# Transposes of q and x on TensorE in halves of eight blocks instead of transposing transfers, and all sums of w_in in group 0

## The chip, the cores and the metric

The kernel runs on one core of a Trainium2 chip. The metric is the device time of one execution in microseconds (us), as the median of several runs. Inside the core, TensorE (PE in the profile, its weight loads PEld) multiplies, VectorE (DVE) and ScalarE (ACT) work on elements, GpSimd (POOL) fills and casts, SyncE (SP) issues most transfers. Each engine takes its own instructions in order; semaphores tie them together.

## The reference

A linear attention with 8 batches, 8 heads, 576 tokens and 64 features a head, and on its output a feed-forward layer with tanh-GELU:

```python
def phi(x):
    return np.where(x > 0, x, np.exp(x) - 1.0) + 1.0
q_p, k_p = phi(q), phi(k)
kv = np.einsum('bhsd,bhse->bhde', k_p, v)
z = np.sum(k_p, axis=2)
num = np.einsum('bhsd,bhde->bhse', q_p, kv)
den = np.einsum('bhsd,bhd->bhs', q_p, z)[..., None] + 1e-06
attn_out = num / den
...
x = attn_out.transpose(0, 2, 1, 3).reshape(4608, 512)
h = x @ w_in                                  # w_in: 512 x 2048
g = 0.5 * h * (1.0 + np.tanh(c * (h + 0.044715 * h * h * h)))
return g @ w_out                              # w_out: 2048 x 512
```

All inputs and the output are float32.

## The kernel before

**Groups.** The 4608 tokens are nine groups of 512. Groups 0 to 7 are the first 512 tokens of the eight batches, four chunks of 128; group 8 is the 64 tokens that are left of each batch ("rest"). `iteration(j)` computes the feed-forward layer of group j and, meanwhile, the attention of group j + 1 and the maps of q and k of batches after it. The order of everything in a group is written out by hand, a string for each group, `ORDER_A` (group 0) to `ORDER_I` (group 8), read word by word. All instructions of an engine stand in the order of these words.

**The words that matter.** `p3` is a plain product for a block of 128 of the 2048 features (4 matmuls of 512 columns) and `g3` its GELU; `X`, `Y`, `Z`, `W` with a number or a letter are the steps of a `Quad`, a product of two by two blocks with seven instead of eight multiplications (matmuls of 256 columns), where `1` to `7` are products on TensorE, `s`, `m`, `u` copies out of PSUM, `c` and `a` additions and `g11` to `g22` GELUs; `o1` to `o7` are the same for w_out, 16 matmuls of 256 columns each, with `os`, `om`, `ou`, `oc..` for their copies and additions; `S1:0-8` are sums of g on VectorE; `n2` is the attention of chunk 2 of the next group: four matmuls of transposed q with the batch's 64x65 blocks of k and v, then a reciprocal and a multiplication on VectorE (`divide`, L290), which leaves a chunk of x with tokens on partitions; `k3` sums k times v for batch 3; `!qe:4`, `!qx:4`, `!qm:4` are the three parts of phi for q of batch 4 (exponential on ScalarE, linear part and minimum on VectorE), `!ke`, `!kx`, `!km` the same for k, `!re`, `!rx`, `!rm` for the rest; `!vc` casts v; `!lq`, `!lk`, `!lv`, `!lr` start loads; `!xs` takes the four sums of the next group's x on VectorE (`sum_x`, L979); `!w0` to `!w3` take the four sums of w_in for the blocks of quad X, Y, Z or W (`sum_w_in`, L956, four VectorE instructions of 512 columns each). A prime moves a copy to the other of ScalarE and VectorE.

**Transposes before.** TensorE contracts over partitions, so q must stand with features on partitions for the attention and x for the product with w_in. Batches 0 and 1 are transposed by TensorE (`transpose_q`, L405 and L510, and `transpose_x`, L346: a matmul of each 128x128 block with an identity, and a copy of PSUM to SBUF). For batches 2 to 7, the rest, and x of groups 2 to 8, `least_q` (L619), `least_rest` (L565) and `transposed_x` (L641) issue transfers from SP that transpose a chunk of 128x512 each: 24, 4 and 28 of them. They stand in SP's queue among the loads, which SP takes in order.

**Buffers.** A pool of seven load buffers (tag `ld`) holds q, k and v of a batch, the float32 weights before their cast, and later three tiles that stay: A and B, which hold sums of w_out and of w_in for the blocks of quads W and X (`begin_sums`, `more_sums`, words `!bq` and `!mq` in group 1), and `rows` (`!br` in group 2). Quads Y and Z have their sums in `w_near`. w_in's sums are taken in group 0 for Y and Z (`!w1`, `!w2`) and at the head of group 3 for X and W (`!w0`, `!w3`). PSUM has six single banks (tag `b`) for all products and TensorE transposes, and one pair (tag `a`) for the attention.

**Group 0.** `first_batch` (L395) brings batch 0 to its x with filler matmuls (`warm`) in between. POOL casts w_in and most of w_out to fp16 as their loads land. `plan_second` (L496) puts batch 1 between the products of group 0: at slot 15 of `ORDER_A` its maps (`maps`, L500), at slot 23 its transposes of q, at 27 its k times v, at 29 to 35 the attention and the transposes of x.

Of the kernel before, what the change touches and what calls it, by code (L numbers as in the profile page):

```python
# [17 lines left out]
def kernel(  # L18
# [9 lines left out]

# [6 lines left out]
    P = 128  # L39
# [40 lines left out]
    def bank(name, shape, dt=FP32):  # L80
        return ps_b.tile(shape, dt, name=name, tag="b")
# [3 lines left out]

# [65 lines left out]

    nc.scalar.preload_act_table_set("exp_and_others")
# [9 lines left out]
    for i in (2, 1, 3):  # L162
        load_w_in(i)
    load_w_out(0)
# [17 lines left out]

    warm = pg.tile([P, 512], BF16, name="warm", tag="g")
    nc.vector.memset(warm, 0.0)
    ident = pth.tile([P, P], BF16, name="ident")
    make_identity(nc, ident)
    vps = [pkv.tile([P, J * NP, E], BF16, name=f"vp{i}") for i in range(2)]
    ident_x = pth.tile([P, P], FP16, name="ident_x")
    t_sum = pth.tile([P, 3, KM // 2, MAIN // 2], FP16, name="t_sum")
    kvbds = [pkv.tile([P, NP, 2 * E], BF16, name=f"kvbd{b}") for b in range(B)]  # L190
    make_identity(nc, ident_x)
    for i in range(2):
        nc.gpsimd.memset(vps[i][:, :, D:E], 1.0)
    for t in kvbds:
        nc.gpsimd.memset(t, 0.0)

# [4 lines left out]

    phi, exps, own = {}, {}, {}
# [44 lines left out]

# [137 lines left out]
    def xt_chunk(j, c):  # L385
        return xts[j][:, :, P * c : P * (c + 1)]
# [5 lines left out]

# [90 lines left out]

# [12 lines left out]
    def plan_second():  # L496
# [3 lines left out]
        def maps():  # L500
            for n in "qk":
                exp_of(n, b)
            cast_w_out(2, nc.scalar.copy, slice(0, 2))
            linear_of("q", b)
            sum_w_out(slice(0, 1))
            linear_of("k", b)
            for n in "qk":
                least_of(n, b)
# [56 lines left out]
    def least_rest(m):  # L565
        least_of("qr", m)
        if m == 0:
            qts[B] = pt.tile([P, C, NP, P], BF16, name="qt")
        nc.sync.dma_start_transpose(
            out=qts[B][:, m], in_=phi["qr", m][:, 0].rearrange("p h d -> p (h d)")  # L570
        )
# [5 lines left out]
    def load_rests(i):  # L577
# [32 lines left out]
        "bq": lambda j: begin_sums(),  # L610
        "mq": lambda j: more_sums(),
# [7 lines left out]
    def least_q(b, cs=slice(0, C)):  # L619
        least_of("q", b, cs=cs)  # L620
        if b not in qts:
            qts[b] = pt.tile([P, C, NP, P], BF16, name="qt")
        for c in range(cs.start, cs.stop):
            nc.sync.dma_start_transpose(
                out=qts[b][:, c],
                in_=phi["q", b][:, c].rearrange("p h d -> p (h d)"),
            )
# [13 lines left out]
    def transposed_x(b, c, x):  # L641
        if b not in xts:
            xts[b] = pt.tile([P, NP, MAIN], FP16, name="xt")
        nc.sync.dma_start_transpose(out=xt_chunk(b, c), in_=x)

    x_parts = {}

    def attention_piece(b, c, in_banks=False):

        if b < B:  # L650
            return transposed_x(b, c, (nab_in_banks if in_banks else nab)(qts[b], b, c))
# [27 lines left out]
        transposed_x(b, c, x)  # L679
# [36 lines left out]


# [205 lines left out]
    FIRST_BLOCK = (0, 2, 4, 6)  # L923
    def sums_at(u, t):
        own["sums"][u] = t.rearrange("p (u n c) f -> p u n c f", u=1, c=KM // 2)
        own["w"][u] = own["sums"][u][:, 0]

    own["w"], own["sums"] = {}, {}
    for u in (1, 2):
        sums_at(u, w_near[:, u])  # L930

    def begin_sums():

        own["A"] = pld.tile([P, MM + 2, N2], FP16, name="w_sum", tag="ld")
        sums_at(3, own["A"][:, MM // 2 : MM])

    def more_sums():

        own["B"] = pld.tile([P, MM + 2, N2], FP16, name="w_more", tag="ld")
        own["qr", 0] = own["B"][:, MM:].rearrange("p a n -> p (a n)").bitcast(BF16)  # L940
        sums_at(0, own["B"][:, MM // 2 : MM])

# [122 lines left out]
    def iteration(j):  # L1065
# [10 lines left out]
        for word in ORDERS[j].split():  # L1076
# [27 lines left out]
            elif kind == "k":  # L1104
                kv_in_pair(int(name))
            elif kind == "S":
# [4 lines left out]
            elif kind == "!":  # L1111
                what, _, b = name.rstrip("'").partition(":")
                if what == "vc":
                    cast_v_of(int(b), name.endswith("'"))
                elif b:
                    prepare_of[what](int(b))
                else:
                    prepare[what](j)
# [5 lines left out]
        "p0 g0 p1 g1 p2 g2 p3 g3 p8 g8 p9 g9 p10 g10 p11 g11 !w1 p4 g4 p5 g5 p6 g6 p7 g7 p12 g12 "  # L1124
        "p13 g13 p14 g14 p15 g15 !w2 @15 o0:0-4 o1:0-4 o2:0-4 o3:0-4 o0:4-8 o1:4-8 o2:4-8 o3:4-8 "
        "@23 o0:8-10 o1:8-10 o2:8-10 o3:8-10 @27 o0:10-12 o1:10-12 @29 o2:10-12 o3:10-12 o0:12-16 "
        "@32 o1:12-16 @33 !qe:2 o2:12-16 @34 o3:12-16 @35"
    )
    ORDER_B = (
        "p0 !ke:2 p13 !lk:3 p1 !kx:2 !vc:2' !km:2 !t !qx:2 @2 p7 !qm:2 p2 g0 !bq !lv:3 !mq g1 g2 "  # L1130
        "p3 g3 k2 !a0 !a2 !a3 p6 p4 p5 p8 g4 p11 g5 !kxb:3 p9 g6 g7 T0-8 o1 os' g8 g9 p10 !qx:3 "
        "!kxa:3 g10 p12 o7 !lk:4 g11 p14 g12 g13 om S1:0-6 p15 S2:0-5 g14 g15 n1' o2 S1:6-8 "
        "S2:5-8 S4:0-6 n0 oc11' o6 !qe:3 n3' ou S4:6-8 !ke:3 n2 o5 oc22 !lq:4 !km:3 !vc:3 o4 oc21 "
        "o3 oc12' !qm:3 !ke:4 !xs !kx:4"
    )
    ORDER_C = (
        "!br k3 @1 Y1 Z1 !km:4 p6 Zs p0 !lk:5 !t g6 !lv:4 Z2 Zg11 Z6 p14 Z7 p8 Zu Z5 Zm g14 p7 g0 "
        "g8 Ys p15 !qx:4 Zc g7 Y6 Yu' Zg22 Y2 Yg11 Y7 Ym Z4 Za g15 n1 p1 g1 Y5 Yc Zg21 Y4 Ya Z3 "
        "Zg12 S1:4-8 n3 o1 Yg22 S2:4-8 p9 S1:0-1 S2:0-1 n2 Yg21 os g9 Y3 Yg12 S1:1-3 S1:3-4 "
        "S2:1-3 S2:3-4 S3:0-8 !qe:4 n0' o2 !lv:5 !qm:4 o6 oc11 ou o7 om o5 !kx:5 S4:0-8 oc22 "  # L1140
        "!ke:5 !vc:4 !xs o4 oc21 o3 !km:5 k4 oc12"
    )
    ORDER_D = (
        "!lq:5 !w0 Z1 X1 !t Y7 Y1 Xs X2 !w3 X7 @1 Ym' X6 Xg11 Ys n1 Xm' Y2 X4 Y6 Xu Xa X5 Yg11 Zs "
        "Xc Yu Xg21 n0 !lk:6 Y4 !vc:5' Z6 Zu X3 Xg12 Z2 Ya Y5 W1 Z7 Yc Zg11 Ws k5 Xg22 Zm Yg21 W6 "
        "Wu' Z5 Yg22 Y3 Yg12 !lv:6 Zc W7 Wm' W2 Z4 Za W5 Zg22 Z3 Wc W4 Wa n3 Wg11 Zg12 Zg21 o1 "
        "S1:0-6 Wg21 n2 os W3 Wg12 S2:0-6 !lq:6 Wg22 S1:6-8 S2:6-8 o2 !qe:5 S3:0-5 o6 S3:5-8 o7 "
        "S4:0-8 !qx:5 ou !qm:5 om !ke:6 oc11 o5 !lk:7 oc22 !vc:6 !kx:6 o4 o3 oc21 !xs oc12'"
    )
    ORDER_E = (  # L1150
        "X1 X7 Xm Xs Y7 !t X6 X2 Xg11 Xu' @1 Y1 Ym X4 X5 Ys Xa Xg21 Z1 Y2 Yg11 Zs !lr:0 Y4 Xc X3 "
        "!km:6 Y6 Yu n2 Z7 Xg12 Z6 Ya Z2 Zu Xg22 Yg21 n1 Zm W1 Z5 Y5 Yc Zc Zg11 Ws k6 Z4 Yg22 W7 "
        "Za Z3 Wm' Zg22 W6 Wu' n3 W4 Zg12 W2 Wg11 Wa Y3 W5 Wc Yg12 S1:0-6 S2:0-6 Zg21 Wg21 o1 os "
        "n0 Wg22 W3 Wg12 S1:6-8 S2:6-8 S3:0-8 !qx:6 o2 !lv:7 S4:0-8 !qe:6 o6 ou !lq:7 oc11 o7 om "
        "!xs o5 oc22 !re:0 o4 !re:1 !ke:7 !qm:6 oc21 !kx:7 o3 oc12'"
    )
    ORDER_F = (
        "!t !km:7 X1 Y1 Y7 !vc:7' Xs Ym' X6 X7 @1 X2 Xu Y4 Xm' !lr:1 X5 Xc X4 Xa Xg11 Ys k7 Y6 "
        "Yu' Y2 Xg22 Xg21 X3 Z1 Yg11 Zs !qx:7 Y5 W1 Yc Z2 Xg12 Ya Zg11 Z6 Zu Ws' Y3 Z7 Zm n1 Yg12 "
        "Z5 Yg22 W6 Wu S1:0-2 W7 Z4 W2 W5 Wm' Zc !rx:0 Zg22 Z3 Zg12 Wc Wg11 n0 Wg22 W4 S1:2-6 "  # L1160
        "S3:0-6 W3 Wg12 o1 os S1:6-8 S3:6-8 S2:0-8 n3 !qe:7 o7 om' o6 Wa Za Zg21 Yg21 ou' n2 o4 "
        "!qm:7 S4:0-6 o5 oc22 Wg21 o2 !rm:0 oc11 S4:6-8 o3 oc21 oc12 !xs"
    )
    ORDER_G = (
        "X1 n0 !rx:1 !rm:1 Xs Y7 Ym' X7 Xm' X2 X6 Xu' Xg11 Y1 Ys X4 Xa n2 X5 Y2 Z1 Xg21 Y6 Y4 "
        "Yg11 Zs W1 Xc Xg22 Yu' Ya !rx:2 X3 Xg12 Yg21 Y5 @1 Z6 Yc Z2 Z7 Zg11 Zu' Ws' Y3 Z5 Yg22 "
        "W7 Wm' W2 Wg11 Yg12 Zm Zc W6 Wu' W4 Zg22 Wa Z3 Zg12 Z4 W5 Za Zg21 Wc S1:0-6 o1 Wg21 "
        "S2:0-6 os n1 W3 Wg22 Wg12 S1:6-8 S2:6-8 S3:0-8 n3' o2 !rx:3 o6 o7 oc11' !re:2 ou S4:0-8 "
        "om o5 !re:3 !rm:2 oc22 o4 oc21 !rm:3 o3 !xs oc12' !t"
    )  # L1170
    ORDER_H = (
        "X1 Xs X7 Xm' n0' n1 X6 Xu X2 Xg11 X4 Y1 Xa X5 Y7 Xc Ys Y6 Xg21 Y2 Yg11 Yu' Z1 X3 W1 Zs "
        "Y5 Z6 Z2 Xg12 Ym Yc Y4 @1 Z7 Zu' Z5 Xg22 Zg11 Ya Y3 Ws W6 W2 Zm Yg21 Zc W7 Yg22 Wu' Wm "
        "Zg22 Wg11 Z3 Zg12 W5 Z4 Za Yg12 Zg21 Wc Wg22 W4 Wa S1:0-6 o1 os W3 Wg21 S2:0-6 Wg12 "
        "S1:6-8 S2:6-8 S3:0-8 n2 n3' o2 oc11 o6 ou o7 om o5 S4:0-8 o4 oc22 !xs o3 oc21 oc12'"
    )
    ORDER_I = (
        "X1 Y7 Ym X7 Xm Xs X2 Xg11 @1 X6 Y1 X4 Z1 Ys Y6 Xu' Xa Xg21 Y2 Y4 Yg11 Zs X5 Yu' Ya Y5 "
        "Yg21 Z7 Z2 Z6 W1 Xc Xg22 Zg11 Yc Y3 Yg22 Zu' X3 Ws' Z5 W6 Zm Zc Yg12 Wu W2 W7 W5 Wg11 Wm "
        "Zg22 Wc Xg12 Z4 Za Z3 Zg12 W4 Wa W3 Wg12 S1:0-6 S2:0-1 Wg22 o1 S1:6-8 S2:1-8 S3:0-8 o5 "  # L1180
        "Zg21 o6 Wg21 S4:0-8 o7 o2 o4 o3"
# [36 lines left out]
```

## Time and profile before

| | |
|---|---|
| median of 3 runs | 265.94 us (265.37 to 266.69) |
| the profiled execution | 266.18 us, its span 264.4 us |
| TensorE clock granted | 1.0 throughout |
| transposing transfers of x (28) | 2.3 us to landing |
| transposing transfers of q (24) | 4.1 us to landing |
| read from HBM, written | 36.70 MB, 9.44 MB |

The span runs from the first to the last instruction in the trace; the time of an execution is a little longer. Busy times of the engines add up over the span, and an engine that waits is not busy. The transfer engines are busy for 93 to 105% of the first 60 us, when the weights and the first batches come in at 348 to 405 GB/s in stretches of 20 us.

### The profile page before, as it was taken

The page shows a single profiled execution, that of the slowest core. Times are in us where ns is not written, and L with a number is a line of the kernel's source. Part 1 is how long each engine was busy: PE and PEld are TensorE (multiplying, and loading weights), DVE is VectorE, ACT ScalarE, POOL GpSimd, SP SyncE. Part 2 cuts the span into 40 slices and gives each one's busy share as a digit, 9 for nine tenths or more (in the row PEclk, how much of TensorE's full clock was granted, in tenths as well). Part 3 has the DMA queues.
Part 4 walks back from the last instruction along what each step waited for, and adds up shares of the span by engine and source line. Part 5 has one row for each costly group of instructions (what it writes and reads, how often), then busy time and mean ns, then how long its engine had stood idle before and what let it go on. Part 6 is the DMA issues. An engine that isn't in the chain of part 4 may idle for free. (4 is left out here: it accounts for less than half of the span.)

```text
span 264.4 us, 6675 instructions
## 1 busy us (share of the span) xinstructions
PE 257.3 (97%) x2765; PEld 203.0 (77%) x2765; DVE 227.7 (86%) x384; ACT 192.1 (73%) x279; POOL 18.8 (7%) x28
## 2 busy tenths in 40 slices
PE   8999999999999999999999999999999999989994
PEld 2584446446876788888888888989889888878883
DVE  3966497799989999999999999999999788868972
ACT  4768795955988788988898988884876478408810
POOL 8056501000000000000000000000000000000000
PEclk9999999999999999999999999999999999999999
DMA  6999999997969969999697398415620450112004
GB/s 235 402 405 397 409 409 396 407 304 217 222 152 286 327 112 222 346 261 241 191 264 195 57 347 236 82 40 68 174 102 21 126 134 2 24 57 121 2 0 159
DMA packets 59789, 53.90 MB, mean 204 GB/s; under 512 B 35696, under 2 KB 45936, under 8 KB 59760
## 3 DMA queue, kind: packets, MB, share of 16 engines
q1 hardware_dynamic: 56880, 44.57, 58.4%
q10 hardware_dynamic: 2880, 8.91, 9.4%
q8 instruction: 21, 0.34, 0.5%
q14 instruction: 8, 0.07, 0.1%
HBM read 36.70 MB, written 9.44 MB: 175 GB/s over the span
## 5 line engine op out<-in xcount | busy, mean ns | idle before, releaser
L784 PEld LDWEIGHTS <-g 128*128 128x128 f16 x624 | 60.5, 98 | 7.8 <-issue 0.4
L784 PE MATMUL o_ps<-w_out_sb,g 128*128 128x256 f16 x384 | 45.7, 273 | 0.0
L356 PE MATMUL h_ps<-xt,w_in_sb 128*128 128x512 f16 (+2 forms) x212 | 37.3, 327 | 0.0
L999 PEld LDWEIGHTS <-w_in_sb 128*128 128x128 f16 x312 | 30.1, 98 | 5.3 <-issue 1.5
L1014 ACT ACTIVATE g<-hq_ps 128x512 f16<-128x512 f32 x52 | 30.9, 622 | 3.9 <-DVE hq_ps L1027 2.5
L356 PEld LDWEIGHTS <-w_in_sb 128*128 128x128 f16 x212 | 18.0, 98 | 14.8
L784 PEld LDWEIGHTS <-s 128*128 128x128 f16 x272 | 26.5, 98 | 3.5
L376 ACT ACTIVATE g<-h_ps 128x512 f16<-128x512 f32 x40 | 22.2, 604 | 8.6 <-PE h_ps L356 8.3
L296 DVE TENSOR_TENSOR xs<-n_ps,r 128x512 f16<-128x512 f32 (+1 forms) x43 | 25.5, 592 | 1.5
L999 PEld LDWEIGHTS <-w_near 128*128 128x128 f16 x224 | 21.6, 98 | 3.5
L999 PE MATMUL hq_ps<-t_sum,w_near 128*128 128x256 f16 x168 | 24.1, 273 | 0.0
L1027 DVE TENSOR_TENSOR rows<-hq_ps,rows 128x512 f32<-128x512 f32 x26 | 17.6, 685 | 1.9 <-PE hq_ps L999 1.2
L1033 ACT COPY h_ps<-hq_ps 128x512 f32<-128x512 f32 x23 | 13.1, 571 | 8.2 <-PE hq_ps L999 7.7
L905 DVE TENSOR_TENSOR o_sb<-o_ps,o_sb 128x512 f32<-128x512 f32 (+1 forms) x21 | 13.3, 636 | 6.5 <-PE o_ps L784 3.6
L1027 DVE TENSOR_TENSOR hq_ps<-hq_ps,rows 128x512 f32<-128x512 f32 x26 | 17.8, 694 | 1.3 <-PE hq_ps L999 0.7
L230 ACT ACTIVATE k_e<-k_x 128x2304 bf16<-128x2304 f32 (+1 forms) x9 | 17.2, 1913 | 2.2 <-DVE o_sb L905 1.3
L1014 ACT ACTIVATE g<-rows 128x512 f16<-128x512 f32 x26 | 17.0, 652 | 2.4 <-DVE rows L1027 2.3
L1014 ACT ACTIVATE g<-h_ps 128x512 f16<-128x512 f32 x26 | 16.1, 621 | 3.2 <-PE h_ps L999 2.9
L230 ACT ACTIVATE q_e<-q_x 128x2048 bf16<-128x2048 f32 (+1 forms) x9 | 15.5, 1721 | 2.8 <-DMA q_x<-in_q_dram 2.8
L999 PE MATMUL h_ps<-xt,w_in_sb 128*128 128x256 f16 x104 | 15.6, 272 | 1.1 <-ACT h_ps L1033 1.0
L999 PE MATMUL hq_ps<-w_sum,w_in_sb 128*128 128x256 f16 x104 | 15.4, 272 | 0.0
L784 PE MATMUL o_ps<-w_sum,s 128*128 128x256 f16 x128 | 15.3, 273 | 0.0
(113 smaller groups left out, 456.2 us busy)
## 6 DMA issues: line engine op xcount, KB each, us to landing
out_dram<-o_sb ACTq DMA_DIRECT2D x16, 512.0 KB, 3.8
k_x<-in_k_dram SPq DMA_DIRECT2D x7, 1152.0 KB, 9.2
v_x<-in_v_dram SPq DMA_DIRECT2D x7, 1152.0 KB, 9.2
q_x<-in_q_dram SPq DMA_DIRECT2D x6, 1024.0 KB, 9.1
w_st<-in_moe_w_in_dram SPq DMA_DIRECT2D x3, 1024.0 KB, 13.4
q_x<-in_q_dram SPq DMA_DIRECT2D x4, 512.0 KB, 11.6
w_st<-in_moe_w_out_dram SPq DMA_DIRECT2D x2, 1024.0 KB, 12.6
w_st<-in_moe_w_out_dram SPq DMA_DIRECT2D x4, 512.0 KB, 11.1
```

What stands on the lines that cost most here:

```text
L230: nc.scalar.activation(o, i, AF.Exp)
L296: nc.vector.tensor_tensor(x_v, n_v[heads + (slice(0, D),)], r[heads + (None,)].to_broadcast(shape + [D]), op=ALU.mult,)
L356: nc.tensor.matmul(h_ps[:, ts], lhsT=w_in_sb[:, c, P * m : P * (m + 1)], rhs=xt[:, c, ts], start=(c == 0), stop=(c == KM - 1), skip_group_ ...
L376: nc.scalar.activation(g_v, h_v, AF.Gelu_apprx_tanh)
L784: nc.tensor.matmul(ps[t] if type(ps) is list else ps[:, t, :], lhsT=lhs[:, m, P * t : P * (t + 1)], rhs=rhs[:, m, :], start=(first and m = ...
L905: nc.vector.tensor_tensor(out, i0, i1, op=ALU.add)
L999: nc.tensor.matmul(ps[:, f], lhsT=lhs[:, c, P * f : P * (f + 1)], rhs=rhs[:, c], start=(first and f == 0 and c == 0), stop=(c == KM // 2 - 1),
L1014: nc.scalar.activation(g_v, src, AF.Gelu_apprx_tanh)
L1027: add = lambda out, i0, i1: nc.vector.tensor_tensor(out, i0, i1, op=ALU.add)
L1033: on(nc.scalar.copy, nc.vector.tensor_copy)(self.seed, self.b)
```

## The change

The transposing transfers go. Words `!qta:b` and `!qtb:b` transpose the first and second two chunks of q of batch b on TensorE (8 blocks each), `t0` and `t1` the first and second two chunks of the next group's x (8 blocks), `!rt:m` a chunk of the rest (4 blocks). Each takes one single PSUM bank and one copy to SBUF, by ScalarE or, with a prime, by VectorE. `n` only leaves its chunk.

A and B are taken from the load buffers right after the loads of w_in, ahead of w_out's, so that the sums of all four blocks are taken in group 0: `!w0` behind `!w1`, and `sum_w_in(3)` in `maps` of batch 1, between the linear part of q and the first sum of w_out. The block of code that sets up the identities and zeros stands earlier in the file. Orders B to I are new throughout; they hold the same products, sums and loads as before, and the words above.

```diff
+    def tiles_of_sums():
+
+        for n in "AB":
+            own[n] = pld.tile([P, MM + 2, N2], FP16, name="w_" + n, tag="ld")
+            nc.gpsimd.memset(own[n][:, 0, 0:2], 0.0)
+        own["qr", 0] = own["B"][:, MM:].rearrange("p a n -> p (a n)").bitcast(BF16)
+        for u, t in enumerate((own["B"][:, MM // 2 : MM], w_near[:, 1], w_near[:, 2])):
+            sums_at(u, t)
+        sums_at(3, own["A"][:, MM // 2 : MM])
...
     for i in (2, 1, 3):
         load_w_in(i)
+    tiles_of_sums()
     load_w_out(0)
...
             linear_of("q", b)
+            sum_w_in(3)
             sum_w_out(slice(0, 1))
...
     def least_rest(m):
         least_of("qr", m)
-        if m == 0:
-            qts[B] = pt.tile([P, C, NP, P], BF16, name="qt")
-        nc.sync.dma_start_transpose(
-            out=qts[B][:, m], in_=phi["qr", m][:, 0].rearrange("p h d -> p (h d)")
-        )
...
     def least_q(b, cs=slice(0, C)):
         least_of("q", b, cs=cs)
-        if b not in qts:
-            qts[b] = pt.tile([P, C, NP, P], BF16, name="qt")
-        for c in range(cs.start, cs.stop):
-            nc.sync.dma_start_transpose(
-                out=qts[b][:, c],
-                in_=phi["q", b][:, c].rearrange("p h d -> p (h d)"),
-            )
...
-    def transposed_x(b, c, x):
+    def copied(other):
+        return nc.vector.tensor_copy if other else nc.scalar.copy
+
+    def transpose_q_half(b, s, other):
+        if b not in qts:
+            qts[b] = pt.tile([P, C, NP, P], BF16, name="qt")
+        t_ps = bank("t_ps", [P, 2, NP, P], BF16)
+        for c in range(2):
+            for i in range(NP):
+                nc.tensor.transpose(
+                    t_ps[:, c, i, :], phi["q", b][:, 2 * s + c, 2 * i : 2 * i + 2, :], ident
+                )
+        copied(other)(qts[b][:, 2 * s : 2 * s + 2], t_ps)
+
+    def transpose_rest(m, other):
+        if m == 0:
+            qts[B] = pt.tile([P, C, NP, P], BF16, name="qt")
+        t_ps = bank("t_ps", [P, NP, P], BF16)
+        for i in range(NP):
+            nc.tensor.transpose(t_ps[:, i, :], phi["qr", m][:, 0, 2 * i : 2 * i + 2, :], ident)
+        copied(other)(qts[B][:, m], t_ps)
+
+    def transpose_x_half(b, s, other):
         if b not in xts:
             xts[b] = pt.tile([P, NP, MAIN], FP16, name="xt")
-        nc.sync.dma_start_transpose(out=xt_chunk(b, c), in_=x)
+        t_ps = bank("t_ps", [P, NP, 2, P], FP16)
+        for c in range(2):
+            for i in range(NP):
+                x = chunks[b, 2 * s + c][:, P * i : P * (i + 1)]
+                nc.tensor.transpose(t_ps[:, i, c, :], x, ident_x)
+        copied(other)(
+            xts[b][:, :, 2 * P * s : 2 * P * (s + 1)], t_ps.rearrange("p i c n -> p i (c n)")
+        )
...
     ORDER_A = (
-        "p0 g0 p1 g1 p2 g2 p3 g3 p8 g8 p9 g9 p10 g10 p11 g11 !w1 p4 g4 p5 g5 p6 g6 p7 g7 p12 g12 "
+        "p0 g0 p1 g1 p2 g2 p3 g3 p8 g8 p9 g9 p10 g10 p11 g11 !w1 !w0 p4 g4 p5 g5 p6 g6 p7 g7 p12 "
...
     ORDER_B = (
-        "p0 !ke:2 p13 !lk:3 p1 !kx:2 !vc:2' !km:2 !t !qx:2 @2 p7 !qm:2 p2 g0 !bq !lv:3 !mq g1 g2 "
...
+        "!qx:2 !qm:2 p8 !ke:2 p5 !t p1 p0 !qtb:2' !kx:2 g0 p2 g1 g2 !vc:2' p3 g3 !km:2 !lk:3 p11 "
+        "p4 g4 g5 !a0 p7 p6 g6 !a2 g7 !a3 k2 !lv:3 !qta:2 o1 os' g8 @2 p9 p12 p10 !qx:3 g9 n0 "
+        "T0-8 !lk:4 p14 g10 g11 g12 p13 n1 g13 !lq:4 g14 !kxb:3 p15 g15 o7 S1:2-3 S1:1-2 S1:0-1 "
+        "!ke:3 o2 S1:3-8 S2:0-8 om !qe:3 n2' !vc:3 t0 n3 o6 !kxa:3 ou' o4 o5 !qm:3 !qtb:3 S4:0-8 "
+        "oc22 oc21 t1 !km:3 !qta:3' o3 oc12' !xs oc11'"
...
     ORDER_F = (
...
+        "!t !qm:6 X1 Xs' X7 Xm' Y7 Ym !qta:6' X2 Xg11 X6 Y4 Xu' Y1 !km:7 Ys X4 !qtb:6 X5 Xa Xg21 "
...
     ORDER_H = (
...
+        "Zm W2 Wg11 Z4 W5 Wm Zc Zg22 !rm:3 Wc Wg22 Z3 Zg12 !rt:3' W4 Wa W3 Wg12 Za Zg21 o1 os "
+        "S1:6-8 S1:0-6 S2:0-8 S3:0-8 n3' n2 Wg21 t0' o2 o6 o7 ou o5 om oc22 t1 o4 S4:0-8 oc11 !xs "
+        "o3 oc21 oc12'"
...
```

## The prediction

> **What bounds the kernel now.** I read the engine sums first, then the busy time by stretch, the chain that ended last, the waits of TensorE, and last the rows that price a transpose and its copy.
>
> ```profile
> PE 257.3 (97%) x2765; PEld 203.0 (77%) x2765; DVE 227.7 (86%) x384; ACT 192.1 (73%) x279; POOL 18.8 (7%) x28
> ```
>
> TensorE is busy for all but 7 us. "Busy" would still hide waits between matmuls, so the next two views test it: four stretches, cut where the sums of the next x end and so groups 2 to 5 (length, then PE, weight loads, DVE, ACT, POOL, clock, DMA share, GB/s), and everything that a matmul waited for after 20 us.
>
> ```profile
> 80.00:102.50 22.50, 22.50 (x191) 17.90 (x190) 21.91 (x40) 18.91 (x27) 0.00 (x0) 1.00 0.93 247
> 102.50:132.20 29.70, 29.36 (x402) 25.61 (x401) 28.90 (x51) 25.64 (x38) 0.00 (x0) 1.00 1.05 252
> 132.20:154.40 22.20, 22.16 (x276) 19.55 (x275) 21.53 (x36) 19.91 (x33) 0.00 (x0) 1.00 0.71 192
> 154.40:184.80 30.40, 30.34 (x349) 26.61 (x347) 29.54 (x48) 22.71 (x33) 0.00 (x0) 1.00 0.58 139
> ```
>
> ```profile
> PE h_ps L999 <- ACT h_ps L1033: 1.0, 2, 0.8
> PE kv_ps L262 <- DVE k_p L246: 0.5, 1, 0.5
> ```
>
> ```profile
> PEld L278 <- DMA qt<-q_p: 0.2, 1, 0.2
> ```
>
> PE's busy time equals the stretch, the granted clock is 1.00, and a transfer that transposes has held up a weight load once, for 0.2 us. The start times of successive matmuls agree: from 20 us to 260 us the distances that exceed the streamed columns by over 120 ns add up to 3.5 us. So each matmul that is added lengthens the run. DVE is second: in these four rows 101.9 of 104.8 us, 97%.
>
> **The change, part by part.** It adds 12 halves of q with 8 transposes (batches 2 to 7, 96), 4 rest blocks with 4 (16) and 14 halves of x with 8 (112): 224 matmuls of 128 columns, each with its own weight load. The kernel before has the same operation in group 0, for q of batch 1:
>
> ```profile
> 36.98 1.06 PE L516 MATMUL t_ps<-ident,q_p 128*128 128x128 bf16 x16
> 37.87 1.89 PE L709 MATMUL o_ps<-w_out_sb,g 128*128 128x512 f16 x8
> ```
>
> The 1.06 contains the pipeline's tail; what 16 transposes take from the stream is the distance to the next group's start, 37.87 - 36.98 = 0.89 us, 55.6 ns each, weight loads included. 224 x 55.6 ns = **12.45 us**. Nothing hides it: PE has no idle time in the stretches above. The Trainium skill, in "TensorE: Matmul & The Clock Gate", section "Back-to-back issue gap", gives about 81 ns for a stream of 128-column matmuls with a weight load each, which would make 18.1 us and a time 5.7 us later than mine; the row of this trace is the same operation in the same kernel, so I take 55.6.
>
> The copies. ACT gets 5 q halves, 10 x halves and 1 rest block, DVE 7, 4 and 3.
>
> ```profile
> L521 ACT COPY qt<-t_ps 128x1024 bf16<-128x1024 bf16 x2 | 1.9, 1015 | 0.3 <-PE t_ps L516 0.3
> L350 ACT COPY xt<-t_ps 128x512 f16<-128x512 f16 x5 | 2.9, 586 | 1.9 <-PE t_ps L349 1.9
> L350 DVE COPY xt<-t_ps 128x512 f16<-128x512 f16 x2 | 0.8, 425 | 0.4 <-PE t_ps L349 0.4
> ```
>
> ACT: 15 x 1.015 + 0.59 = 15.8 us. DVE has no 1024-wide row: not under the 425 ns of 512 columns, not over twice that; DVE's 16-bit differences go from 418 to 680 ns for the same doubling, so I take 0.69 us: 11 x 0.69 + 3 x 0.425 = 8.9 us (5.9 to 10.6). The new orders also move five evacuations of 512 columns from ACT to DVE: 3.4 us. In groups 2 to 5 (the four rows) PE gains 24 + 40 + 16 + 40 = 120 transposes, 6.7 us, so the stretch grows from 104.8 to 111.5 us. DVE gains 6 copies (4.1) and at most the 3.4, and loses the eight sums that group 3 has now (8 x 0.42 = 3.4): 106.0 of 111.5 us. ACT, 87.2 us there, gains 9 copies: 96.3. Both stay under PE, so copies cost nothing in the sum; without that cover, DVE's share would be the 8.9.
>
> What is removed: 56 transposes from SP's queue, and with them the waits of loads queued behind them. No matmul waits on those loads (the list above), so I count 0 (0 to -0.2, the one wait on such a transfer; DVE waited once, 1.4 us, for a transposed x, which no matmul shows). Where the wait goes: transposes stand in PE's own queue, behind DVE's last map of q or its division of x, and everything of PE stands behind them. In the new orders most have room: in group 7 the second x half comes four products of 16 matmuls, 109 ns each, behind the matmuls that its last division reads: 7.0 us, for a division of 0.9. Tight are the q halves set near their last map (groups 1 and 5): 0 to 1 us each, I take 0.
>
> The sums of w_in for blocks 0 and 3 go from group 3 to group 0. There DVE shares time with POOL's casts:
>
> ```profile
> 20.80 2.09 POOL L141 CAST w_in_sb<-w_st 128x2048 f16<-128x2048 f32 x1 [0.92 <-DMA w_st<-in_moe_w_in_dram]
> ...
> 26.09 2.16 POOL L147 CAST w_out_sb<-w_st 128x2048 f16<-128x2048 f32 x1 [0.85 <-DMA w_st<-in_moe_w_out_dram]
> ```
>
> ```profile
> 20.70 0.42 DVE L969 TENSOR_TENSOR w_near<-w_near,w_in_sb 128x512 f16<-128x512 f16 x1
> 21.16 2.00 DVE L969 TENSOR_TENSOR w_near<-w_in_sb,w_near 128x512 f16<-128x512 f16 x1
> ...
> 26.53 1.99 DVE L969 TENSOR_TENSOR w_near<-w_in_sb,w_near 128x512 f16<-128x512 f16 x1
> ...
> 33.25 1.23 DVE L730 TENSOR_TENSOR w_near<-w_out_sb 128x2048 f16<-128x2048 f16 x1 [3.25 <-POOL w_out_sb L147]
> ```
>
> A sum that begins inside a cast takes 2.0 us instead of 0.42 and ends 0.27 us after the cast (23.16 against 22.89, 28.52 against 28.25). DVE idles 2.1 us before 25.3 and 3.25 us before 33.25, but POOL casts from 23.35 to 25.24 and 31.32 to 33.21, in the same gaps. Block 0's sums then get one in before 23.35 and three after 25.24 (1.25 us); block 2's fall into the cast that ends at 28.25 and end near 30.0 instead of 28.5; the map of q ends at 31.2; of block 3's sums one fits before the cast, three come after 33.25. So the last map of q for batch 1 ends some **1.3 us** later than now, 38.2 against 36.9, and the 16 transposes that PE starts at 36.98 wait for it, with all of group 0's products behind. Bounds: 0, if the loads land so that the sums fall between the casts, to 3.4, all eight sums uncovered.
>
> The two load buffers that these sums take hold up loads of group 0: the first of w_out waits for v's cast instead of q's maps (both over by 12.4 us; its issue is at 12.10), v of batch 1 for a cast of w_out at 28.3 (issued at 26.11 now). By v of batch 2 the queue runs at 400 GB/s, so a bubble there moves a landing that DVE waits 1.0 us for today. Its user is put later in the new group 1. I take 0 (0 to 2).
>
> Sum: span 264.4 + 12.45 + 1.3 = 278.15 us; the profiled execution took 266.18 us, 1.8 more than its span: **279.9 us**. That execution lies 0.24 us over the median of 265.94, within the runs' scatter, so no correction.
>
> **The rivals.**
> *Bank waits.* The six single PSUM banks get 30 more users, and PE waits in order for each bank. For it: DVE at 97% frees banks late. Against: t_ps is taken 13 times up to the end of group 0 now, and PE's list names no wait for a bank there. At 0.2 us each (the size of several entries in the list) it adds 6 us: 286; at 0.1 us, 283.
> *Waits vanish with the reordering.* The 3.5 us of gaps could all go and group 0's sums cost nothing: 266.18 + 12.45 - 3.5 = 275.1; half of it, 276.9.
> *Not slower: the transposing transfers stretch the matmul stream.* Place: the 1624 products of 256 columns (896 with w_out, 728 with w_in), nearly all between 55 and 261 us, while transposing transfers run from 55.7 to 231 us. They start 109 ns apart. If reading and writing the same memory costs them time, it comes back: at 7.7 ns each (12.45 us / 1624) the time is 266.2 again, and from there the kernel would be no slower. Against it: the last products run after the last transposing transfer, and 112 of them still take 109 ns each (12.24 us); and 32 of 512 columns at 30 us, before the first one, take 6.91 us, 216 ns each or 108 for half the columns.
>
> ```profile
> 248.73 12.24 PE o_ps L784 x112
> ```
>
> **How the numbers follow.** Forecast with its bounds (277.5 to 282.5): 0.55. Bank waits: 0.23. Vanishing waits: 0.19. Not slower: 0.02. The last 0.01 is for gains that I can't name. The range goes to half of the vanished waits below and to nearly the whole bank price above: 276.3 to 285.5. A measurement of this kernel tells 0.5% (1.3 us) from no change, and the first three cases lie far beyond that: slower 0.97, same 0.02, faster 0.01.
>
> **What would show it.** Right: PE has 224 more matmuls and stays at 96 to 97% busy; consecutive transposes start 55 to 57 ns apart; the span grows by 12 to 15 us, spread over groups 1 to 7 in proportion to their transposes; DVE stays under PE in every stretch after 80 us; the transposes of batch 1's q start near 38.2 us. Wrong: PE's idle time rises with t_ps or the next bank's owner as the releaser (bank waits); DVE fills a stretch and PE does not (DVE has become the bound); the 256-column products come closer than 109 ns (the transfers did stretch them).

## The result, and the profile after

| | before | after |
|---|---|---|
| median | 266.06 us (265.37 to 266.69) | 276.4 us (275.84 to 276.67) |
| ratio | | 1.0387 [1.0356, 1.0418] |
| profiled execution, its span | 266.18, 264.4 us | 276.67, 274.9 us |
| granted TensorE clock | 1.0 | 1.0 |

The changed kernel is slower by 10.3 us. The forecast was 279.9 us with 276.3 to 285.5 as range: the time lies in the range, at its lower end, and below the 277.5 that the forecast's own bounds allowed. It is 0.1 us above the end of the range, and single runs go from 275.84 to 276.67 us: that it lies inside is partly luck. Medians and ratios in this document are of fast runs; two of the four runs of one kernel below (dma_pool_loads, 320.34 and 330.22 us) were in a slower state of the chip and are left out.

First the engine sums of the changed kernel.

```profile
PE 267.9 (97%) x2988; PEld 215.2 (78%) x2989; DVE 241.1 (88%) x394; ACT 204.7 (74%) x290; POOL 18.4 (7%) x30
```

TensorE has 223 more matmuls in the records (224 were added; single records can be missing), 10.6 us more busy time, and the same share of a longer span. DVE and ACT each gained some 13 us and neither passed PE. The busy time by stretch, cut at the sums of the next x as before (length, then PE, weight loads, DVE, ACT, POOL, clock, DMA share, GB/s), says the same of groups 2 to 5:

```profile
81.80:101.10 19.30, 19.30 (x170) 15.06 (x168) 18.39 (x34) 16.18 (x25) 0.00 (x0) 1.00 0.33 109
101.10:138.00 36.90, 36.90 (x502) 33.34 (x500) 35.45 (x56) 31.24 (x41) 0.00 (x0) 1.00 0.54 171
138.00:161.10 23.10, 23.10 (x294) 20.71 (x292) 22.42 (x36) 20.97 (x33) 0.00 (x0) 1.00 0.50 176
161.10:193.10 32.00, 32.00 (x388) 28.74 (x386) 31.13 (x53) 25.62 (x35) 0.00 (x0) 1.00 0.22 75
```

The four lengths add up to 111.3 us, DVE to 107.4 and ACT to 94.0; the forecast had 111.5, 106.0 and 96.3. The new orders moved work between the four (the second is 7 us longer, the first 3 us shorter), so only the sums compare. DVE is busy for 95 to 97% of each of the four, so it has little room left there.

What matmuls and weight loads waited for after 20 us (engine, line, what for; us in total, times, longest). The first fence holds all that the view lists for matmuls, the second the two lines of weight loads for transposes of q:

```profile
PE h_ps L365 <- ACT g L385: 0.2, 1, 0.2
PE t_ps L524 <- DVE q_p L256: 0.2, 1, 0.2
```

```profile
PEld L524 <- DVE q_p L256: 0.7, 1, 0.7
PEld L644 <- DVE q_p L256: 0.3, 1, 0.3
```

The matmuls' waits on ACT's evacuation of `h_ps` and on k's map, and the weight load's wait on a transposed q, are gone. New are the transposes of q of batch 1 (L524) behind DVE's last map, and one product of group 1 (L365) that waits 0.2 us for a GELU to free its bank. The weight load at L644, in group 1, waited 0.3 us for a map of q, but the product ahead was still streaming, and no gap stands there. No wait names a copy of `t_ps`.

The price of a transpose and of its copy stands in the timeline of PE (start, duration, line, operation; count) and in the groups by shape (busy, mean ns | idle time of the engine before them):

```profile
133.86 0.61 PE L664 MATMUL t_ps<-ident_x,xs 128*128 128x128 f16 x8
134.31 1.06 PE L644 MATMUL t_ps<-ident,q_p 128*128 128x128 bf16 x16
135.20 1.91 PE L812 MATMUL o_ps<-w_out_sb,g 128*128 128x256 f16 x16
```

```profile
L665 ACT COPY xt<-t_ps 128x1024 f16<-128x1024 f16 x10 | 10.0, 1017 | 2.4 <-PE t_ps L664 2.2 <-issue 0.2
L647 DVE COPY qt<-t_ps 128x1024 bf16<-128x1024 bf16 x7 | 4.8, 683 | 0.8 <-PE t_ps L644 0.8
```

Sixteen transposes take 135.20 - 134.31 = 0.89 us, as in group 0 of the kernel before. DVE's copy of 1024 columns takes 683 ns, the estimate was 690.

**Where the 10.5 us of span come from.** I added up, matmul by matmul, the distance to the start of the next one, and called a gap what exceeds the streamed columns by over 120 ns:

| | before | after | difference |
|---|---|---|---|
| added transposes | 0 | 224, 56.8 ns each | +12.71 us |
| gaps after 20 us | 3.47 us (10) | 0.85 us (3) | -2.62 us |
| products of 256 columns | 178.30 us | 177.91 us | -0.39 us |
| start of the first product with w_out | 30.07 us | 30.82 us | +0.75 us |
| sum | | | +10.45 us |

The last step, 0.75 us, isn't put down to the change: the same product starts at 29.98 us in one of the kernels below that have the new group 0, and at 30.81 us in another that has the old one. So the change costs what its transposes take, less the gaps that it loses. Of the 3.47 us of gaps before, the list of matmul waits in the prediction names ACT for 1.0 us and DVE for 0.5; for the other seven gaps, 0.16 to 0.23 us each, it names no engine. After 54 us and before 249 us the changed kernel has no gap at all.

### The profile page after: what moved, and what is told of

It is laid out like the page before. It is cut to its first block, busy times and chain, and to the rows that moved or that the text cites. A ratio compares the mean times of both kernels' runs of the same rounds, so it can differ in the third digit from the quotient of the medians.

```text
span 274.9 us, 7015 instructions
## 1 busy us (share of the span) xinstructions
PE 267.9 (97%) x2988; PEld 215.2 (78%) x2989; DVE 241.1 (88%) x394; ACT 204.7 (74%) x290; POOL 18.4 (7%) x30
## 3 DMA queue, kind: packets, MB, share of 16 engines
q1 hardware_dynamic: 26416, 37.23, 38.2%
## 4 chain that ended last, share of the span: by engine, by line
PE 82%; DVE 6%; DMA 5%; ACT 2%; SPq 2%; POOL 1%; issue 1%
PE o_ps L812 31%; PE hq_ps L1007 25%; PE h_ps L365 6%; DMA w_st<-in_moe_w_in_dram 5%; PE h_ps L812 4%; PE h_ps L1007 4%; PE n_ps L287 2%; PE t_ps L664 2%; PE o_ps L739 2%; PE t_ps L644 2%; PE kv_ps L271 2%; DVE w_B L977 2%; DVE w_near L977 2%; DVE w_A L977 1%; SPq L90 1%; ACT k_e L240 1%
## 5 line engine op out<-in xcount | busy, mean ns | idle before, releaser
L365 PE MATMUL h_ps<-xt,w_in_sb 128*128 128x512 f16 (+2 forms) x212 | 37.8, 327 | 0.2 <-ACT g L385 0.2
L365 PEld LDWEIGHTS <-w_in_sb 128*128 128x128 f16 x212 | 17.9, 98 | 14.6 <-issue 0.5
L812 PE MATMUL o_ps<-w_B,g 128*128 128x256 f16 x128 | 15.3, 273 | 0.0
L812 PE MATMUL o_ps<-w_near,s 128*128 128x256 f16 x128 | 15.3, 273 | 0.0
## 6 DMA issues: line engine op xcount, KB each, us to landing
k_x<-in_k_dram SPq DMA_DIRECT2D x7, 1152.0 KB, 10.6
```

The source lines that it names most:

```text
L365: nc.tensor.matmul(h_ps[:, ts], lhsT=w_in_sb[:, c, P * m : P * (m + 1)], rhs=xt[:, c, ts], start=(c == 0), stop=(c == KM - 1), skip_group_ ...
L812: nc.tensor.matmul(ps[t] if type(ps) is list else ps[:, t, :], lhsT=lhs[:, m, P * t : P * (t + 1)], rhs=rhs[:, m, :], start=(first and m = ...
```

## The experiments

Twelve kernels ran in three groups, each group beside the kernel before on the same chip (medians 266.35, 265.51 and 266.12 us). Excess is the median over that of its own group; the changed kernel's is 10.3 us. Gaps are counted as above, after 20 us of the profiled execution.

| kernel | median, us | ratio to before | excess, us | gaps of PE, us |
|---|---|---|---|---|
| changed kernel | 276.40 | 1.0387 [1.0356, 1.0418] | 10.3 | 0.85 |
| sums_only | 265.83 | 0.9995 [0.9979, 1.001] | -0.5 | 2.47 |
| dma_new_orders | 295.46 | 1.1113 [1.1076, 1.115] | 29.1 | 26.4 |
| x_dma | 290.62 | 1.0929 [1.0895, 1.0964] | 24.3 | 18.2 |
| q_dma | 279.32 | 1.0501 [1.0467, 1.0535] | 13.0 | 7.9 |
| twice_tr | 288.46 | 1.0857 [1.0832, 1.0883] | 22.9 | 0.53 |
| twice_cp | 285.24 | 1.0737 [1.0717, 1.0757] | 19.7 | 9.4 |
| pe_old_orders | 349.59 | 1.3152 [1.3098, 1.3205] | 84.1 | 60.7 |
| dma_pool_loads | 315.39 | 1.187 [1.1806, 1.1933] | 49.9 | 47.5 |
| twice_cp_act | 282.61 | 1.0629 [1.0606, 1.0653] | 16.5 | 7.6 |
| twice_cp_dve | 280.75 | 1.0559 [1.054, 1.0578] | 14.6 | 4.9 |
| copies_act | 281.92 | 1.0603 [1.0584, 1.0622] | 15.8 | 5.9 |
| sums_late | 279.14 | 1.0499 [1.0479, 1.0518] | 13.0 | 3.3 |

My theory was: TensorE is full, so the cost is its 224 transposes; the copies are covered; the gaps went because nothing waits for transfers any more. The rivals were that the new orders alone removed the gaps, and that the early sums did.

**The transposes doubled (twice_tr).** Each added transpose is issued twice; the second writes the same values.

```diff
-        for c in range(2):
+        for c in (0, 1, 0, 1):
             for i in range(NP):
```

> The changed kernel with each of the 224 added transposes done twice into the same place, copies once: 224 more matmuls of 128 columns and nothing else. My theory: TensorE has no room, so each costs its 57 ns again: 276.4 + 12.7 = 289.1 us, within 1 us. Rival: part of the transposes lies in time in which TensorE would wait anyway (a bank, a map, a division): clearly under, by as much as they are covered.

Measured: 288.46 us, an excess 12.6 us larger than the changed kernel's, 56.3 ns for each of the 224. Its engine sums:

```profile
PE 280.7 (98%) x3213; PEld 228.2 (80%) x3213; DVE 242.0 (84%) x394; ACT 205.0 (71%) x290; POOL 18.9 (7%) x30
```

PE is busy 12.8 us longer, DVE and ACT by less than 1 us, and one gap is left. So PE's time is the path from end to end, and a transpose costs its 56 ns. This is the row that the forecast took. The Trainium skill, in "TensorE: Matmul & The Clock Gate", section "Back-to-back issue gap", has about 81 ns for 128 columns in a stream with weight loads; here the sustained distance is 56.3 to 56.8 ns with a weight load each, and the measurement decides.

**The copies doubled, on both engines, on ACT alone, on DVE alone (twice_cp, twice_cp_act, twice_cp_dve).** All 30 copies, ACT's 16, or DVE's 14 are done twice (the diff is of the first kernel):

```diff
-        copied(other)(qts[b][:, 2 * s : 2 * s + 2], t_ps)
+        for _ in range(2):
+            copied(other)(qts[b][:, 2 * s : 2 * s + 2], t_ps)
```

> The changed kernel with each copy of a half or rest block from PSUM done twice (15.8 us more on ScalarE, 8.9 us more on VectorE), transposes once. My theory: both engines have room and each bank is held 0.7 to 1.0 us longer; hidden but for a few waits: 276.4 to 279 us. Rival: the copies or the banks they hold are on the path; then 282 to 290 us.

Measured: 285.24 us, 9.4 us over the changed kernel by excess. The theory's 0 to 2.6 us fell, and the time is in the rival's range. I had read "covered" as "has room", and that is not the same. Then one engine at a time:

> The changed kernel with ScalarE's 16 copies of transposes done twice, VectorE's once. Doubling all cost 8.8 us (285.2). Theory A: ScalarE's queue is the thin cover, since a copy of 1.0 us stands there ahead of copies and GELUs that free banks: 6 to 9 us of the 8.8, 282 to 285 us. Theory B: VectorE, 97% busy in the middle, is: under 3 us here, 276.4 to 279.4.

> The changed kernel with VectorE's 14 copies of transposes done twice, ScalarE's once. Theory A (ScalarE is the thin cover): 276.4 to 279 us. Theory B (VectorE is): 6 to 9 us more, 282 to 285 us.

Measured: 282.61 and 280.75 us, that is 6.2 us more for ACT's copies and 4.3 us for DVE's, together about what both cost in one kernel. ACT's lies in theory A's range; DVE's lies between the two theories, so neither foresaw that both engines are thin. The longest waits of PE in the first and in the second of these:

```profile
PE o_ps L815 <- ACT o_sb L914: 1.6, 2, 1.4
PE h_ps L365 <- ACT xt L668: 0.9, 1, 0.9
PE hq_ps L1010 <- ACT qt L648: 0.8, 1, 0.8
```

```profile
PE hq_ps L1010 <- DVE rows L1053: 0.9, 2, 0.7
PE o_ps L815 <- DVE g L775: 0.8, 2, 0.5
PE hq_ps L1010 <- DVE t_sum L998: 0.7, 1, 0.7
```

Two of the lines, 1.7 us on ACT (`xt`, `qt`), are waits for the doubled copies themselves. The others are waits behind evacuations, GELUs and sums that have nothing to do with transposes: the added copies stand ahead of these in the engine's queue and make them late. By their mean times in the changed kernel ACT's second copies are 15.8 us of work and DVE's 8.8, so ACT costs 0.39 us and DVE 0.49 us for each us of copying; per us the busier engine (DVE 88%, ACT 78% of its span) is the dearer one, and ACT's larger total comes from its longer copies. What decides how much of a copy is hidden, no run tests by itself; my reading is that it is the number of matmuls between a copy and the first one behind it that waits for the same engine.

**All copies on ACT (copies_act).**

```diff
     def copied(other):
-        return nc.vector.tensor_copy if other else nc.scalar.copy
+        return nc.scalar.copy
```

> The changed kernel with all 30 copies of transposes on ScalarE (8.9 us off VectorE, 13 us more on ScalarE). Theory A (ScalarE's queue is thin): 2 to 6 us slower than the changed kernel, 278.4 to 282.4 us. Theory B (VectorE is): the same or up to 1 us faster, 275.4 to 276.6 us.

Measured: 281.92 us, 5.5 us more, in theory A's range, though ACT goes only to 77% and DVE falls to 83%. PE waits for ACT's evacuations of `h_ps` (1.2 us in three, 1.1 us in two). With the copies split over two engines the transposes cost no more than their columns; on one they do.

**The early sums alone (sums_only), and the late sums in the new kernel (sums_late).** The first is the kernel before with A and B taken early and all sums of w_in in group 0; orders and transfers stay. The second is the changed kernel with the sums for X and W back at the head of group 3. The diff is of the first.

```diff
+    tiles_of_sums()
     load_w_out(0)
...
-        "p0 g0 p1 g1 p2 g2 p3 g3 p8 g8 p9 g9 p10 g10 p11 g11 !w1 p4 g4 p5 g5 p6 g6 p7 g7 p12 g12 "
+        "p0 g0 p1 g1 p2 g2 p3 g3 p8 g8 p9 g9 p10 g10 p11 g11 !w1 !w0 p4 g4 p5 g5 p6 g6 p7 g7 p12 g12 "
...
-        "!lq:5 !w0 Z1 X1 !t Y7 Y1 Xs X2 !w3 X7 @1 Ym' X6 Xg11 Ys n1 Xm' Y2 X4 Y6 Xu Xa X5 Yg11 Zs "
+        "!lq:5 Z1 X1 !t Y7 Y1 Xs X2 X7 @1 Ym' X6 Xg11 Ys n1 Xm' Y2 X4 Y6 Xu Xa X5 Yg11 Zs "
```

> The kernel before with one part of the change alone: the two load buffers taken early and all sums of w_in in group 0; old orders, transposes by transfers. My theory: group 0 ends 0.4 to 1.3 us later (TensorE waits for the last map of batch 1's q), group 3 loses two waits of 0.6 us together and 3.4 us of VectorE work, which TensorE does not feel: 265.5 to 267.0 us, same. Rival: the sums in group 3 caused the waits that the change removed; then 263.5 us.

Measured: 0.9995, no difference, as expected. DVE's last map of q for batch 1 in this kernel (start, duration):

```profile
35.70 1.22 DVE L264 TENSOR_TENSOR q_p<-q_p,q_e 128x2048 bf16<-128x2048 bf16 x1
```

It ends at 36.92 us, where the kernel before has 36.88: in this execution the eight more sums went into DVE's idle time and moved nothing. Of the two waits at the head of group 3 that the theory took off (gaps of 0.23 and 0.40 us), gaps of 0.14 and 0.41 us are still there.

> The changed kernel with the sums of w_in for quads X and W back at the head of group 3, their buffers still taken early. My theory: group 0 gains at most the 0.5 us for which TensorE waits for the last map of batch 1's q; group 3 gets 3.4 us of VectorE work in a stretch in which VectorE is 97% busy and the orders count on it: 277 to 280 us. Rival: the place of the sums does not matter here either, as with the old orders: 276.0 to 276.8 us.

Measured: 279.14 us, 2.7 us more, as the theory had it. PE's two waits over 1 us:

```profile
PE hq_ps L1006 <- DVE w_B L976: 1.4, 1, 1.4
PE hq_ps L1006 <- DVE rows L1049: 1.1, 1, 1.1
```

So the place of the sums is worth nothing with the old orders, and 2.7 us with the new ones, in which group 3 has transposes and copies and no slack for 3.4 us of DVE. The rival that the early sums alone removed the gaps is out: sums_only keeps 2.47 of the 3.47 us. The 1.0 us that it lost may be theirs; that is one profiled execution each.

**The transfers back in the new orders (dma_new_orders, x_dma, q_dma).** The changed kernel, with x and q, x alone, or q alone transposed by transfers that are issued where the kernel before issues them, behind the division or the last map; the words for TensorE transposes do nothing.

```diff
+    def transposed_x(b, c, x):
+        if b not in xts:
+            xts[b] = pt.tile([P, NP, MAIN], FP16, name="xt")
+        nc.sync.dma_start_transpose(out=xt_chunk(b, c), in_=x)
...
             elif kind == "t":
-                transpose_x_half(j + 1, int(name[0]), name.endswith("'"))
+                pass
```

> The changed kernel with all 56 transposes given back to transfers (issued where the kernel before issues them: behind the last map of q and behind each chunk of x), in the new orders, sums of w_in in group 0. My theory: the 224 TensorE transposes are the whole loss (12.7 us of matmul starts in the changed kernel's trace), and the 2.6 us of TensorE waits that are gone went with the new orders; then the time is 276.4 - 12.7 = 263.7 us, under the kernel before, or up to 2 us more where a transfer lands later than its reader stands. Rival: the waits of the kernel before came from the transposing transfers and from SP's queue; then they come back and the time is 266 us or more.

> The changed kernel with x alone transposed by transfers (112 TensorE transposes fewer). My theory, 57 ns for each: 276.4 - 6.4 = 270.0 us, within 1 us. Rival, costs sit in q's or x's copies, banks or waits and not in the count: clearly off 270, and not the same as the run with q by transfers.

> The changed kernel with q and the rest alone transposed by transfers (112 TensorE transposes fewer). My theory: the same 270.0 us, within 1 us. Rival: as for x by transfers.

Measured: 295.46, 290.62 and 279.32 us. All three theories fell; the rivals' numbers held, but the waits that came are new and far larger than those of the kernel before. Taking TensorE's transposes away makes this kernel slower, by 19 us for all. Where dma_new_orders loses most, SP's queue and DVE read:

```profile
183.00 1.22 SPq L690 DMA_TRANSPOSE xt<-xs  x1
184.32 0.53 SPq L99 DMA_DIRECT2D q_x<-in_q_dram  x1
```

```profile
182.25 0.69 DVE L305 TENSOR_TENSOR xs<-n_ps,r 128x512 f16<-128x512 f32 x1
189.62 1.23 DVE L248 TENSOR_SCALAR q_p<-q_x 128x2048 bf16<-128x2048 f32 x1 [6.68 <-DMA q_x<-in_q_dram]
```

The load of q for batch 7 (L99) stands behind a transpose of x that waits for DVE's division; it goes out at 184.32 us, and DVE's next instruction, the first map of that q, waits for it for 6.68 us. DVE's queue stands, and with it the copies that empty PSUM:

```profile
PE hq_ps L1023 <- DVE rows L1066: 6.9, 2, 6.3
PE n_ps L287 <- DMA qt<-q_p: 3.7, 2, 2.4
```

In the changed kernel the same load leaves SP's queue at 157.14 us:

```profile
157.14 0.37 SPq L99 DMA_DIRECT2D q_x<-in_q_dram  x1
```

The new order of group 5 has `!lq:7 !qx:7`, the load right ahead of its user; in the old orders over forty words stand between the two. Without transposing transfers in its queue SP comes to that load 27 us earlier. x_dma shows the same waits (DVE 6.9, PE 6.3 us); in q_dma the longest wait of DVE for a load of q is 1.8 us. So it is x's transfers, issued behind the division, that hold SP ahead of this load. PE's wait there is one of several, 6.3 of the 26.4 us of gaps. In q_dma PE waits 3.1 us for transposed q instead.

**TensorE transposes in the old orders (pe_old_orders).** The kernel before, with a transpose of two chunks on PE wherever it issues the transfers for them, all copies on ACT, and `t_ps` in the pair of banks.

```diff
     def transposed_x(b, c, x):
-        if b not in xts:
-            xts[b] = pt.tile([P, NP, MAIN], FP16, name="xt")
-        nc.sync.dma_start_transpose(out=xt_chunk(b, c), in_=x)
+        chunks[b, c] = x
+        if (b, c ^ 1) in chunks:
+            transpose_x_half(b, c // 2, False)
```

> The kernel before, its orders kept, with the 56 transposing transfers replaced by the same 224 TensorE transposes at the places where the transfers were issued, that is right behind the last map of q or the division of the second chunk of x; in the pair of banks, all copies on ScalarE. My theory: TensorE now stands behind VectorE at each of the 30 places, 0.5 to 1.5 us each, 15 to 30 us in all on top of 12.7: 294 to 309 us; so the new orders are a part of the change that the transposes need. Rival: the place does not matter and the time is that of the changed kernel, 276 to 280 us.

Measured: 349.59 us, 84.1 us over before; the direction was right, the size far too small. What PE waited for:

```profile
PE t_ps L661 <- DVE xs L296: 29.9, 15, 4.5
PE t_ps L641 <- DVE q_p L246: 7.5, 4, 3.9
PE t_ps L641 <- ACT qt L644: 6.6, 6, 1.1
```

Here a transpose that stands right behind its division or its map stops PE until DVE is done, 2.0 us on average behind a division (29.9 us in 15), and everything of PE stands behind it. The new orders put most transposes some products later, which is part of what the rewritten strings do. The kernel differs from the changed one in the engine of the copies and in the banks as well, so 84 us is not the price of the orders alone.

**The loads in another queue (dma_pool_loads).** To part "SP's queue blocks loads" from "the transfer itself is late", dma_new_orders with the later loads issued by POOL.

```diff
-        nc.sync.dma_start(out=ld[name, b][:, us, :], in_=s[:, us, :])
+        (nc.gpsimd if b > 2 else nc.sync).dma_start(out=ld[name, b][:, us, :], in_=s[:, us, :])
```

> The run with all transposes by transfers in the new orders (295.5 us), with the loads of q from batch 4, of k and v from batch 3 and of the rests issued from POOL's queue instead of SP's. Theory A: the 26.4 us of TensorE waits there come from loads that stand in SP's queue behind transposing transfers which wait for VectorE; freed, the time falls to 275 to 284 us. Theory B: they come from the transfers' own time (four in a row, 1.2 us each to issue and 2.3 to 4 us to land) in front of readers that stand too near; then it stays over 289 us.

Measured: 315.39 us, over theory B's 289. It decides nothing, because the edit changed what it was to hold still. The transposing transfers of q and of x in dma_new_orders and in this kernel (count, median us to landing), and what PE waited for in the latter:

```profile
xt<-xs SPq DMA_TRANSPOSE x28, 3.4
qt<-q_p SPq DMA_TRANSPOSE x24, 3.3
```

```profile
xt<-xs SPq DMA_TRANSPOSE x28, 2.3
qt<-q_p SPq DMA_TRANSPOSE x24, 9.3
...
PE n_ps L287 <- DMA qt<-q_p: 32.9, 7, 10.4
```

The transposing transfers of q became three times as slow, those of x faster. Whether free loads would have helped with q's transfers at their former speed stays open.

## Why the prediction was right, and where it was off

- *PE is the bound, 224 transposes cost their columns: 12.45 us.* Shown. 12.71 us in the trace, 12.6 us by doubling. The step carried the result.
- *The copies cost nothing.* Right for this kernel: no matmul waits for a copy of `t_ps`. But the price given for lost cover, DVE's 8.9 us, was about twice too high for DVE and left out ACT: the second set of copies cost 4.3 us through DVE and 6.2 us through ACT.
- *DVE and ACT stay under PE in groups 2 to 5.* Right, as the four stretches show.
- *What is removed counts 0.* This is the step that failed, with the sentence "with them the waits of loads queued behind them. No matmul waits on those loads". It counted only waits on transfers. The gaps that existed, 1.5 us of them named as waits on ACT and DVE and the rest unnamed, fell from 3.47 to 0.85 us. The mechanism "waits vanish with the reordering" was on the list as a rival at 275.1 us for all of them and 276.9 us for half; 276.4 us lies between. With 2.6 us off, the forecast's sum is 277.3 us. So the forecast's own case (277.5 to 282.5 us, chance 0.55) did not come; the time is one of the rival with 0.19, and that rival's part of the range made the range hold. The sign "the span grows by 12 to 15 us" failed mainly for the same reason: it grew by 10.5.
- *Group 0's sums delay q's transposes by 1.3 us.* The mechanism was right, the term was mis-sized: the sums make TensorE wait 0 to 0.7 us. In the profiled execution of the changed kernel the last map ends at 38.02 us, as predicted (38.2), but PE reaches the transposes late too:

```profile
38.08 1.07 PE L524 MATMUL t_ps<-ident,q_p 128*128 128x128 bf16 x16 [0.18 <-DVE q_p L256]
```

Of the 1.10 us by which they start later than before, 0.75 are the late start of the products and 0.35 the wait (563 ns from the product ahead, where 512 columns take 216). Eleven of the kernels here have this group 0, the changed one among them. In seven the wait is nil, in four it is 0.35 to 0.71 us; the last map ends anywhere from 36.92 to 38.02 us. The two kinds differ in when POOL begins its last cast of 128x1024 of w_in: at 16.9 to 17.3 us in the seven, where the sums begin at 18.6 to 18.8, and at 18.3 to 18.9 us in the four, where they begin at 19.9 to 20.5 and more of them fall into later casts. The kernel before belongs to the second kind (18.31); x_dma, with the cast at 18.30 us, starts the transposes at 37.60 instead of 36.98 us, so between like executions the sums cost 0.6 us. In the seven the products with w_out start 0.7 us later than in the kernel before, which covers the sums. The forecast took the kind of execution that its trace showed, and placed the last map 0.7 us too late for that kind (38.2 us, where x_dma has 37.54).
- *Tight q halves and two load buffers: 0.* Right: a weight load waits once, 0.3 us, for a map of q in group 1, and no matmul waits for either.
- *Bank waits.* One of 0.2 us in the changed kernel, behind a GELU; they are what copies_act produces, with PE waiting for ACT's evacuations.
- *Not slower, because transposing transfers stretch the matmul stream.* Out: products of 256 columns take 109.6 ns without such transfers and 109.9 with them. The last 112 read the same in both kernels:

```profile
259.22 12.24 PE o_ps L812 x112
```

Two questions stay open. Which of the vanished gaps went because of the free SP queue, and which because of the new order of words, isn't parted: each method of transposing in the other's orders makes new and larger gaps (26.4 and 60.7 us), so neither swap isolates a cause. And how much of dma_new_orders' loss is the blocked queue and how much the late transfers of q isn't told apart. No version tried here beats the kernel before; sums_only equals it.

## What to carry to other kernels

When TensorE is full, a transpose on it costs its columns, however well the copies are hidden; count them first (224 x 56 ns), and look for the gain only in waits that the timeline already shows. The Trainium skill's rule in "VectorE: DVE Perf Modes", section "Rules for kernel authors", says to transpose on TensorE where the result may go to PSUM. In this kernel, with TensorE busy 97% of the span, doing so cost 10.3 us. An order of instructions written for one method of transposing isn't neutral ground for comparing it with another: either swap alone was worse than both tuned kernels, by 19 us or more where everything was swapped.

## What the runs showed of the hardware

**The granted clock fell after a long wait.** Busy time by stretch around the 6.3 us wait of dma_new_orders (columns as above):

```profile
184.50:187.00 2.50, 0.70 (x9) 0.55 (x7) 0.00 (x0) 1.17 (x3) 0.00 (x0) 1.00 0.61 159
187.00:194.00 7.00, 2.50 (x12) 1.78 (x12) 4.34 (x7) 0.59 (x2) 0.00 (x0) 0.73 0.30 104
194.00:200.00 6.00, 5.72 (x42) 4.36 (x40) 3.71 (x8) 3.58 (x7) 0.00 (x0) 0.75 0.51 116
200.00:206.00 6.00, 6.00 (x59) 5.32 (x56) 5.73 (x12) 3.90 (x4) 0.00 (x0) 1.00 0.38 68
```

The clock falls in the stretch in which PE waits, and from 194 to 200 us, with PE at work again, it is still at 0.75 on average, so the wait costs more than its length. The mean clock was 1.0 in twice_cp with 9.4 us of gaps, none of them over 1.6 us, 0.977 in dma_new_orders with 26.4 us and 0.936 in pe_old_orders with 60.7 us.

**With the later loads in POOL's queue the transposing transfers of q landed later:** 9.3 instead of 3.3 us (median), while those of x landed in 2.3 instead of 3.4 us. Why the two differ, no run shows.

**A sum on DVE that began inside a POOL cast took 2.0 us instead of 0.42.** The trace of before had this (21.16 and 26.53 us), and the changed kernel has four such sums in group 0. Among the eleven kernels with the new group 0, the last map of q ends up to 1.1 us apart.
